# Token and state loads of later batches rearranged over two DMA queues, and one batch's attention chain placed two steps earlier

## The chip, the cores and the metric

The kernel runs on one core of a Trainium2 chip. The metric is the device time of one execution in microseconds (us). Before the change the median of three runs is 204.96 us (204.93 to 205.63).

## The reference

Eight batches of cross attention between 512 tokens and 32 state vectors per head (8 heads of width 64), in both directions, then one feed-forward layer over all 8 × 544 rows:

```python
scores = scale * x @ state.T            # [B, H, 512, 32], softmax over the 32 states
xread  = softmax(scores) @ state        # [B, H, 512, 64]
scores2 = scale * state @ x.T           # [B, H, 32, 512], softmax over the 512 tokens
sread  = softmax(scores2) @ x           # [B, H, 32, 64]
rows   = concat([xread, sread], axis=2) # to [B * 544, 512]
h = rows @ w_in                         # w_in [512, 2048]
out = maximum(0.01 * h, h) @ w_out      # w_out [2048, 512]
```

Inputs and output are fp32.

## The kernel before

The kernel works in bf16 on TensorE with fp32 sums. It does not form `xread`: for each batch it first multiplies the states with w_in (`a_m`, the matrix M, four column groups of 512, each copied out of PSUM by `m_evict`), so that the first feed-forward matmul is attention weights times M.

The order of the instructions on each engine is written out by hand; nothing is scheduled afterwards. SP and Pool each issue DMAs from their own instruction stream, in order, and an instruction that has to wait holds what is behind it.

Per batch the work is:
- load of the tokens, fp32 (`load_x`, tile `xl`, one buffer for all batches from 2 on), a cast to bf16 (`cast_x`), and a DMA transpose by SP (`a_xt_dma`, tile `xT`);
- states: `load_state(i)` loads a group of batches (group 0: batches 2 and 3, group 1: batches 4 to 7) with eight small DMAs; `state_t(i)` casts on Pool and transposes by DMA on SP (`st_t`);
- `a_scores` on TensorE into the PSUM tile `sc`; `a_shift` (maxima per row, their transposed spread and the subtraction, on DVE), `a_max2` (maxima of the second softmax), `a_exp` and `a_exp2` on ScalarE (ACT), `a_probs` and `a_probs2` on DVE, which end in the attention weights `aT` and `a2`;
- 16 steps of the first feed-forward matmul (`ff1`, `ff1_pair`): each fills a PSUM bank `ph`, and ACT applies the leaky ReLU into `hT`. `ff1_pair` does two steps in the double bank `big`, which M groups use too;
- the second feed-forward matmul. For batches 0 and 1 it is cut into `piece(b, hT, i, jq)`: quarter jq of the sum for row block i, four matmuls with quarter jq of `w_out`. Later batches use seven products of half size in place of eight (`Batch`, `Fast`).

The steps of one batch are interleaved with the attention of the next and the second matmul of the one before. The change touches the start. The weights are cast in flight by DMAs of Pool in quarters: `w_in` in four (`load_w_in`), `w_out` in four (`load_w_out`). Pool's queue at the start is, in order: the four of w_in, a cast of batch 0, the first quarter of w_out, two halves of batch 1's tokens (`x1`), quarters two to four of w_out, and batch 2's tokens (`load_x(2)`). SP's queue begins with batch 0's tokens in two halves (`xf`); then come the states of batches 2 and 3, held by a small DVE write into their tile that stands behind DVE's casts of batch 1.

Batch 0's attention and first matmul run to about 22 us, then the pieces of batch 0 with w_out's quarters in turn, between which batch 1's transposes, scores and M groups lie. Then comes the loop of 16 steps of batch 1's first matmul, in which at step 5 batch 2's scores and first M group are formed, at step 9 its exp and weights, at steps 11 and 13 its second exp. ACT copies the M group out, and DVE takes one of the output copies.

Of the kernel before, what the change touches and what calls it, by code (L numbers as in the profile page):

```python
# [9 lines left out]
P = 128  # L10
B, H, S, D = 8, 8, 512, 64
# [4 lines left out]
NT = S // P  # L16
NK = H // 2
# [3 lines left out]
FP32 = mybir.dt.float32  # L21
# [6 lines left out]
def kernel(  # L28
# [9 lines left out]
    nc = tc.nc  # L38
# [58 lines left out]
    def load_x(b, eng):  # L97
        xl[b] = xpool.tile([P, H, NT * D], FP32, name="xl", tag="xl", bufs=1)
        eng.dma_start(xl[b][:], x[b].rearrange("h (p t) d -> p h (t d)", t=NT))

    def open_xb(b):
        xs[b] = xpool.tile([P, NT, H, D], BF16, name="xb", tag="xb")

    def cast_x(b, h0, h1, copy):
        copy(  # L105
            xs[b][:, :, h0:h1].rearrange("p t h d -> p h t d"),
            xl[b][:, h0:h1].rearrange("p h (t d) -> p h t d", t=NT),
        )
# [54 lines left out]
    stf = [consts.tile([P, hi - lo, P], FP32, name=f"stf{lo}", tag=f"stf{lo}") for lo, hi in groups]  # L163
    stb = [consts.tile([P, hi - lo, P], BF16, name=f"stb{lo}") for lo, hi in groups]

    def load_state(i):
        lo, hi = groups[i]
        for k in range(NK):
            for g in range(2):
                nc.sync.dma_start(  # L170
                    stf[i][NS * k:NS * (k + 1), :, D * g:D * (g + 1)],
                    state[lo:hi, 2 * k + g].rearrange("b n d -> n b d"),
                )

    def state_t(i):
        POO(stb[i][:], stf[i][:])
        nc.sync.dma_start_transpose(st_t[i][:], stb[i][:].rearrange("p b q -> p (b q)"))
# [6 lines left out]
    def a_open(a, b):  # L184
        a.b = b
        a.xb = xs[b]
        a.xT = att.tile([P, NT, NK, P], BF16, name="xT", tag="xT")
# [69 lines left out]
    def a_exp(a):  # L257
        a.e1 = block_exp(a.sh, NB)
# [5 lines left out]
    def a_max2(a):  # L264
        m2 = att.tile([P, 2], FP32, name="mcol", tag="mcol")
        nc.vector.tensor_reduce(out=m2[:], in_=a.sc[:], axis=AX.X, op=ALU.max, negate=True)  # L266
        a.m2s = att.tile([P, 2], FP32, name="mcols", tag="mcols")
        nc.vector.tensor_scalar(out=a.m2s[:], in0=m2[:], scalar1=SCALE, scalar2=None, op0=ALU.mult)
# [484 lines left out]
    for u in range(2):  # L753
        nc.gpsimd.dma_start(
            x1[u][:], x[1, NK * u:NK * (u + 1)].rearrange("h (p t) d -> p h (t d)", t=NT)
        )
    for c in range(1, 4):
        load_w_out(c)
    load_x(2, nc.gpsimd)
    a0.aT = att.tile([P, 2, S], BF16, name="aT", tag="aT")  # L760
    open_xb(1)
    a_open(a1, 1)
# [63 lines left out]
    for j, tag in ((4, "py"), (6, "sc"), (8, "py"), (10, "ph"), (12, "py"), (14, "ph")):  # L826
        t, bk = open_ff1_0(tag)
        for g in range(2):
            ff1_0(bk, j, g)
        relu0(t, j)  # L830
        if j == 8:
            m_evict(a0, 3, a_m(a0, 3, "big"), VEC)
            a_scores(a0)
            a_max2(a0)
    for u in range(2):
        VEC(
            a1.xb[:, :, NK * u:NK * (u + 1)].rearrange("p t h d -> p h t d"),
            x1[u][:].rearrange("p h (t d) -> p h t d", t=NT),
        )
    nc.vector.memset(stf[0][:, 0, D - 1:D + 1], 0.0)  # L840
    load_state(0)

    for g in range(2):
        a_exp2(a0, g)
# [18 lines left out]
        piece(0, h0, i, 1)  # L863
    m_evict(a1, 2, a_m(a1, 2, "ph"), SCA)
    a_exp(a1)
    for i in (2, 3):
        piece(0, h0, i, 1)
    m_evict(a1, 3, a_m(a1, 3, "ph"), SCA)
    for g in range(2):
        a_exp2(a1, g)  # L870
    open_xb(2)
    state_t(0)
    cast_x(2, 0, 4, SCA)
    cast_x(2, 4, 8, POO)
    a_open(a2, 2)
    a_xt_dma(a2)
    load_x(3, nc.sync)
    open_xb(3)
    a_probs(a1)
# [15 lines left out]
    for s in range(16):  # L895
        if s in (6, 10):
            ff1_pair(a1, h1, s, "big")
        elif s not in (7, 11):
            ff1(a1, h1, s)
        if s == 5:  # L900
            a_scores(a2)
            m_evict(a2, 0, a_m(a2, 0, "big"), SCA)
            a_shift(a2)
            a_max2(a2)
        if s % 2:
            pb, hT, i, jq = fill[s // 2]
            piece(pb, hT, i, jq, copy=VEC if s == 3 else SCA)
        if s == 7:
            a_open(att_of[3], 3)
            a_xt_dma(att_of[3])  # L910
        elif s == 9:
            a_exp(a2)
            a_probs(a2)
        elif s in (11, 13):
            a_exp2(a2, s // 2 - 5)
    a_probs2(a2)
    a_probs2(a1)
    a_a2t(a1)
    pm = [a_m(a2, 1, "big"), a_m(a2, 2, "sc")]
    m_evict(a2, 1, pm[0], VEC)  # L920
    m_evict(a2, 2, pm[1], SCA)

# [2 lines left out]
    for b in range(2, B):  # L927
        hT = hpool.tile([P, 16, S], BF16, name="hT", tag="hT")
        a = att_of[b]
        nxt = att_of[b + 1] if b + 1 < B else None  # L930
        now = Batch(b, hT)
        std = []
        if b == 2:
            std = [(i, 3) for i in range(2)] + [(i, jq) for i in range(2, NT) for jq in range(4)]

        def fill(s):
            n = (PACE2 if b == 2 else PACE)[s]
            left = min(n, len(before.units)) if before else 0
            if left:
                before.run(left)  # L940
            if n > left:
                now.run(n - left)

        for s in range(16):
            if s == 11:
                fill(s)
            ff1(a, hT, s)
            if s == 0:
                if b + 2 < B:
                    load_x(b + 2, nc.sync)  # L950
                    open_xb(b + 2)
                a_a2t(a)
                if before:
                    for n in (0, 1):
                        before.f.sums(n, 4, 8)
            elif s == 1:
                if nxt is not None:
                    a_scores(nxt)
                m_evict(a, 3, a_m(a, 3, "big"), SCA)
                if b == 2:  # L960
                    a_sread_rows([a0])
                if nxt is not None:
                    a_shift(nxt)
                if b + 2 < B:
                    for h in range(0, H, 2):
                        cast_x(b + 2, h, h + 2, POO)
                if before:
                    before.f.sums(2, 4, 8)
            elif s == 3:
                if before:  # L970
                    before.f.sums(3)
                if nxt is not None:
                    a_max2(nxt)
                if b == 2:
                    weights_sum(0)
                    weights_sum(2)
            elif s == 4:
                if b == 2:
                    load_state(1)
                elif b == 4:  # L980
                    sread_t(0, 4)
                elif b == 7:
                    sread_t(1, 3)
            elif s == 8:
                if nxt is None:
                    a_sread(a)
                if b == 2:
                    state_t(1)
                    weights_sum(1)
                    weights_sum(3)  # L990
            elif s == 12:
                for n in range(3):
                    now.f.sums(n, 0, 4)
            if nxt is None:
                if s == 4:
                    fi = FastIn(None)
                    for n in range(3):
                        fi.w_sum(n)
                elif s == 10:
                    fi.w_sum(3)  # L1000
                    fi.x_sums()
            if s == (11 if b == 2 else 7) and b + 2 < B:
                a_open(att_of[b + 2], b + 2)
                a_xt_dma(att_of[b + 2])
            if nxt is not None:
                if s == 5:
                    a_exp(nxt)
                elif s in (7, 8):
                    a_exp2(nxt, s - 7)
                    if s == 7:  # L1010
                        a_probs(nxt)
                elif s == 11:
                    a_probs2(nxt)
                elif s in (12, 13):
                    SCA(nxt.M[:, s - 12, DM:2 * DM], pm1[:, s - 12, :])
            if std:
                i, jq = std.pop(0)
                piece(1, h1, i, jq)
            elif s != 11:
                fill(s)  # L1020
            if s == 10 and nxt is not None:
                a_sread_rows([a1, a2] if b == 2 else [a])
                pm0 = a_m(nxt, 0, "big")
                pm1 = a_m(nxt, 1, "sc")
                pm2 = a_m(nxt, 2, "ph")
                for g, copy in enumerate((VEC, SCA)):
                    copy(nxt.M[:, g, 2 * DM:3 * DM], pm2[g][:])
                m_evict(nxt, 0, pm0, SCA)
        before = now
# [90 lines left out]
```

## Time and profile before

| | |
|---|---|
| median of three runs | 204.96 us |
| the profiled execution | 204.74 us |
| its span | 202.9 us |
| granted TensorE clock | 1.0 |
| TensorE busy | 196.8 us, 97% |
| DVE, ACT, Pool busy | 75%, 71%, 21% |
| moved by DMA | 28.0 MB, 138 GB/s over the span |
| landing of batch 2's tokens after issue | 19.1 us |
| landing of a quarter of w_out, median | 16.9 us |

The span runs from the first to the last instruction on the engines; the profiled execution's own time is 1.8 us longer. A line of a timeline gives the start, the length of the merged group, engine, source line, operation, output <- input, the number of instructions and in brackets the idle time before it and what ended that. PE is TensorE, PEld its weight loads. A DMA's row on an issuing engine is the time of its issue; the landing stands in a part of its own. Matmul ends are modelled, so the distance of starts says more than the busy time.

### The profile page before, as it was taken

To read this page: it belongs to the slowest core of one execution; us is meant where nothing else is said; L and a number is where in the kernel's file an instruction comes from. 1 tells how busy PE (TensorE), PEld (TensorE's weight loads), DVE (VectorE), ACT (ScalarE), POOL (GpSimd) and SP (SyncE) were. 2 spreads that over 40 slices of the span, in tenths; PEclk is the share of its full clock that TensorE was granted. 3 is DMA by queue.
4 is the path that set the end of the run, shared out by engine and by line. 5 is a ranking of instruction groups with operands and counts; after the bars stand their busy time and mean duration, and the time that the engine had idled before them with its cause. 6 is when DMAs were issued, how large, how long until landed. Compare 5 with 4: busy or idle time off the path is not lost.

```text
span 202.9 us, 4755 instructions
## 1 busy us (share of the span) xinstructions
PE 196.8 (97%) x1964; PEld 125.7 (62%) x1964; DVE 152.7 (75%) x231; ACT 143.3 (71%) x264; POOL 42.3 (21%) x66
## 2 busy tenths in 40 slices
PE   7989999999999999999999999999999999999993
PEld 2543534434344567766776767776767677799882
DVE  1767689689999969976997699769968853686612
ACT  3558748579869796978797878788778856467710
POOL 8931002022007004400251040200020002004250
PEclk9999999999999999999999999999999999999999
DMA  5999994799396986538946795250017000410035
GB/s 187 227 207 277 229 252 131 147 304 236 64 265 190 104 183 159 103 117 256 122 30 181 236 131 105 103 158 5 0 50 213 18 0 28 182 55 0 3 89 170
DMA packets 39733, 27.99 MB, mean 138 GB/s; under 512 B 25312, under 2 KB 36704, under 8 KB 39712
## 3 DMA queue, kind: packets, MB, share of 16 engines
q1 hardware_dynamic: 34512, 20.88, 42.9%
q0 software_dynamic: 4912, 6.55, 15.8%
q8 instruction: 15, 0.25, 0.5%
q10 hardware_dynamic: 288, 0.26, 0.5%
q14 instruction: 6, 0.05, 0.1%
HBM read 17.30 MB, written 8.91 MB: 129 GB/s over the span
## 4 chain that ended last, share of the span: by engine, by line
PE 89%; DMA 5%; POOL 2%; ACT 1%; DVE 1%; issue 0%; POOLq 0%
PE yq L557 36%; PE ph L372 23%; PE py L487 10%; DMA w_in_bf<-in_moe_w_in_dram 5%; PE pm L351 4%; PE pyw L487 3%; PE pf L441 3%; PE yu L557 3%; PE ph L803 2%; PE psn L318 1%; PE sc L206 1%; PE phw L383 1%; POOL w_in_bf L118 1%; DVE M L365 1%; ACT hT L377 1%; ACT M L365 1%
## 5 line engine op out<-in xcount | busy, mean ns | idle before, releaser
L377 ACT ACTIVATE hT<-ph 128x512 bf16<-128x512 f32 x108 | 63.6, 604 | 22.0 <-PE ph L372 21.5
L372 PE MATMUL ph<-aT,M 128*128 128x512 bf16 x216 | 62.3, 379 | 0.0
L557 PEld LDWEIGHTS <-su 128*128 128x128 bf16 x416 | 39.7, 98 | 14.5 <-DVE su L546 1.7
L557 PEld LDWEIGHTS <-hT 128*128 128x128 bf16 x288 | 27.7, 98 | 11.8 <-issue 1.1
L105 POOL CAST xb<-xl 128x512 bf16<-128x512 f32 (+1 forms) x21 | 16.4, 818 | 61.1 <-DMA xl<-in_x_dram 61.1
L557 PE MATMUL yq<-tw_xf,su 128*128 128x256 bf16 x192 | 27.2, 273 | 0.0
L557 PE MATMUL yq<-w_out_bf,hT 128*128 128x256 bf16 x192 | 27.0, 273 | 0.0
L372 PEld LDWEIGHTS <-M 128*128 128x128 bf16 x216 | 21.0, 98 | 9.1 <-DVE r L280 0.4
L546 DVE TENSOR_TENSOR su<-hT 128x1024 bf16<-128x1024 bf16 x24 | 16.9, 702 | 10.5 <-ACT hT L377 10.5
L487 PE MATMUL py<-w_out_bf,hT 128*128 128x512 bf16 x96 | 24.2, 380 | 0.0
L487 PEld LDWEIGHTS <-hT 128*128 128x128 bf16 x128 | 12.0, 98 | 14.8 <-issue 1.3
L627 POOL TENSOR_TENSOR yo<-sv,sv 128x512 f32<-128x512 f32 x6 | 7.8, 1300 | 52.8 <-ACT sv L566 41.3
L569 DVE TENSOR_TENSOR yo<-yq,sv 128x512 f32<-128x512 f32 x17 | 11.6, 685 | 6.5 <-PE yq L557 6.5
L566 ACT COPY sv<-yq 128x512 f32<-128x512 f32 x24 | 13.9, 585 | 2.0 <-PE yq L557 1.4
L365 ACT CAST M<-pm 128x1024 bf16<-128x1024 f32 x13 | 13.2, 1014 | 0.6 <-PE pm L351 0.6
L557 PE MATMUL yq<-w_out_bf,su 128*128 128x256 bf16 x96 | 13.1, 273 | 0.0
L557 PE MATMUL yq<-tw_x,su 128*128 128x256 bf16 x96 | 13.1, 273 | 0.0
L557 PE MATMUL yq<-tw_x,hT 128*128 128x256 bf16 x88 | 12.1, 273 | 0.0
L274 ACT ACTIVATE e<-sc,mcols 128x512 bf16<-128x512 f32 x16 | 11.1, 696 | 0.0
L216 DVE TRANSPOSE_TENSOR_REDUCE mrow<-sc 128x32 f32<-128x1024 f32 x7 | 8.7, 1243 | 1.4 <-PE sc L206 1.4
L266 DVE TENSOR_REDUCE mcol<-sc 128x2 f32<-128x1024 f32 x8 | 9.7, 1214 | 0.0
L224 DVE STREAM_TRANSPOSE mrowb<-mrow 128x1024 f32<-128x1024 f32 x7 | 8.7, 1245 | 0.2
(148 smaller groups left out, 271.5 us busy)
## 6 DMA issues: line engine op xcount, KB each, us to landing
xl<-in_x_dram SPq DMA_DIRECT2D x5, 1024.0 KB, 6.8
out_dram<-yo SPq DMA_DIRECT2D x10, 512.0 KB, 2.8
w_in_bf<-in_moe_w_in_dram POOLq DMA_DIRECT2D x4, 512.0 KB, 8.9
w_out_bf<-in_moe_w_out_dram POOLq DMA_DIRECT2D x4, 512.0 KB, 16.9
out_dram<-ysb SPq DMA_DIRECT2D x8, 256.0 KB, 5.4
xf<-in_x_dram SPq DMA_DIRECT2D x2, 512.0 KB, 4.8
x<-in_x_dram POOLq DMA_DIRECT2D x2, 512.0 KB, 14.0
xl<-in_x_dram POOLq DMA_DIRECT2D x1, 1024.0 KB, 19.1
```

Of the source, the lines that this page charges most:

```text
L105: copy(xs[b][:, :, h0:h1].rearrange("p t h d -> p h t d"), xl[b][:, h0:h1].rearrange("p h (t d) -> p h t d", t=NT),)
L216: nc.vector.tensor_reduce(out=m1[:], in_=flat.rearrange("p (c j) -> p c j", j=NS), axis=AX.X, op=ALU.max, apply_transpose=True,)
L266: nc.vector.tensor_reduce(out=m2[:], in_=a.sc[:], axis=AX.X, op=ALU.max, negate=True)
L274: nc.scalar.activation(out=a.e2[:, g], in_=a.sc[:, g, :], func=AF.Exp, bias=a.m2s[:, g:g + 1], scale=SCALE, accum_out=a.r2[:, g:g + 1],)
L365: copy(a.M[:, :, cols], pm[:])
L372: nc.tensor.matmul(ph[:], lhsT=a.M[:, g, P * j:P * (j + 1)], rhs=a.aT[:, g, :], start=(g == 0), stop=(g == 1),)
L377: nc.scalar.activation(out=hT[:, j, :], in_=ph[:], func=AF.Prelu, alpha=0.01)
L487: nc.tensor.matmul(y.py, lhsT=hT[:, j, P * i:P * (i + 1)], rhs=w_out_bf[:, j, :], start=(j == 0), stop=(j == 15),)
L546: (eng or nc.vector).tensor_tensor(out=S[n][:, ms], in0=u[:, ms], in1=v[:, ms], op=op)
L557: nc.tensor.matmul(bank[:, i, :], lhsT=lhs[:, m, P * i:P * (i + 1)], rhs=rhs[:, m, :], start=(first and m == 0 and (i == 0 or of is not No ...
L566: copy(t[:], bank)
L569: nc.vector.tensor_tensor(out=dst, in0=bank, in1=self.sv[n][:], op=ALU.add)
```

## The change

- Batch 2's tokens no longer stand at the end of Pool's queue. They are loaded by SP in two halves, right behind batch 0's tokens, and are held by a small DVE write into their tile, which stands after batch 0's second maxima and ahead of batch 1's casts.
- The eight loads of the states of batches 2 and 3 move from SP to Pool, between batch 1's tokens and w_out's second quarter. Their DVE write is dropped.
- The casts of batch 2 (ACT, Pool) and its transpose move up: on ACT the cast now stands behind batch 1's exp, ahead of its last M copies and second exps.
- In batch 1's loop the scores and first M group of batch 2 go from step 5 to step 3, its exp and weights from step 9 to 7, its second exps from 11 and 13 to 9 and 11. The output copy of step 3 goes from DVE to ACT.
- The states of batches 4 to 7 are loaded in that loop, four DMAs at step 5 and four at step 9, in place of step 4 of the next one; their cast and transpose move from step 8 to step 4 there. Batch 4's token transpose goes from step 11 to 9.
- After the loop, the normalisation `a_probs2` and transpose of batch 1's second softmax stand behind the two M copies of batch 2.

```diff
-    def load_state(i):
+    def load_state(i, ks=range(NK), eng=nc.sync):
...
-        for k in range(NK):
+        for k in ks:
...
-                nc.sync.dma_start(
+                eng.dma_start(
...
         nc.gpsimd.dma_start(
             x1[u][:], x[1, NK * u:NK * (u + 1)].rearrange("h (p t) d -> p h (t d)", t=NT)
         )
+    load_state(0, eng=nc.gpsimd)
     for c in range(1, 4):
         load_w_out(c)
-    load_x(2, nc.gpsimd)
...
             a_scores(a0)
             a_max2(a0)
+    xl[2] = xpool.tile([P, H, NT * D], FP32, name="xl", tag="xl", bufs=1)
+    nc.vector.memset(xl[2][:].rearrange("p h q -> p (h q)")[:, NK * NT * D - 1:NK * NT * D + 1], 0.0)
+    for u in range(2):
+        nc.sync.dma_start(
+            xl[2][:, NK * u:NK * (u + 1)],
+            x[2, NK * u:NK * (u + 1)].rearrange("h (p t) d -> p h (t d)", t=NT),
+        )
...
-    nc.vector.memset(stf[0][:, 0, D - 1:D + 1], 0.0)
-    load_state(0)
+
+    state_t(0)
...
     a_exp(a1)
+    open_xb(2)
+    cast_x(2, 0, 4, SCA)
+    cast_x(2, 4, 8, POO)
+    a_open(a2, 2)
+    a_xt_dma(a2)
     for i in (2, 3):
         piece(0, h0, i, 1)
     m_evict(a1, 3, a_m(a1, 3, "ph"), SCA)
     for g in range(2):
         a_exp2(a1, g)
-    open_xb(2)
-    state_t(0)
-    cast_x(2, 0, 4, SCA)
-    cast_x(2, 4, 8, POO)
-    a_open(a2, 2)
-    a_xt_dma(a2)
...
-        if s == 5:
+        if s % 2:
+            pb, hT, i, jq = fill[s // 2]
+            piece(pb, hT, i, jq)
+        if s == 3:
             a_scores(a2)
             m_evict(a2, 0, a_m(a2, 0, "big"), SCA)
             a_shift(a2)
             a_max2(a2)
-        if s % 2:
-            pb, hT, i, jq = fill[s // 2]
-            piece(pb, hT, i, jq, copy=VEC if s == 3 else SCA)
         if s == 7:
+            a_exp(a2)
+            a_probs(a2)
             a_open(att_of[3], 3)
             a_xt_dma(att_of[3])
-        elif s == 9:
-            a_exp(a2)
-            a_probs(a2)
-        elif s in (11, 13):
-            a_exp2(a2, s // 2 - 5)
+        elif s in (9, 11):
+            a_exp2(a2, s // 2 - 4)
+        if s in (5, 9):
+            load_state(1, range(s // 2 - 2, s // 2))
     a_probs2(a2)
-    a_probs2(a1)
-    a_a2t(a1)
     pm = [a_m(a2, 1, "big"), a_m(a2, 2, "sc")]
     m_evict(a2, 1, pm[0], VEC)
     m_evict(a2, 2, pm[1], SCA)
+    a_probs2(a1)
+    a_a2t(a1)
...
                 if b == 2:
-                    load_state(1)
+                    state_t(1)
...
-                    state_t(1)
...
-            if s == (11 if b == 2 else 7) and b + 2 < B:
+            if s == (9 if b == 2 else 7) and b + 2 < B:
```

## The prediction

> **What bounds the kernel now.** I read the page first.
>
> ```profile
> span 202.9 us, 4755 instructions
> ...
> PE 196.8 (97%) x1964; PEld 125.7 (62%) x1964; DVE 152.7 (75%) x231; ACT 143.3 (71%) x264; POOL 42.3 (21%) x66
> ```
>
> TensorE is busy 97% of the span, and the change alters no matmul, only their order. So it can win no more than the holes in PE's row, and any matmul that it makes wait costs its full wait: PE takes its instructions in order, and everything behind it shifts. Second I read PE's timeline for holes in the stretch that the change touches, then ACT's beside it.
>
> ```profile
> 40.82 0.41 PE L206 MATMUL sc<-xT,st_t 64*32 64x512 bf16 x8
> 41.03 0.41 PE L351 MATMUL pm<-w_in_bf,st_t 64*32 64x512 bf16 x8
> 41.38 1.04 PE L487 MATMUL py<-w_out_bf,hT 128*128 128x512 bf16 x4
> 42.64 1.02 PE L383 MATMUL phw<-aT,M 128*128 128x512 bf16 x4 [0.22 <-ACT M L365]
> 43.50 1.03 PE L487 MATMUL py<-w_out_bf,hT 128*128 128x512 bf16 x4
> ...
> 41.57 1.01 ACT L365 CAST M<-pm 128x1024 bf16<-128x1024 f32 x1
> ```
>
> Four matmuls of this shape occupy 0.86 us from start to start (42.64 to 43.50), so the group of 41.38 should hand over at 42.24; phw starts at 42.64. That hole of 0.40 us is the largest between 20 and 66 us: phw needs the bank "big", which ACT's copy of batch 2's M frees at 42.58. This is what "two steps up" can win.
>
> Third I read Pool's queue, since the change puts eight transfers into it.
>
> ```profile
> 3.00 3.18 POOL L118 DMA_DIRECT2D w_in_bf<-in_moe_w_in_dram  x4
> ...
> 7.38 0.75 POOL L124 DMA_DIRECT2D w_out_bf<-in_moe_w_out_dram  x1
> 8.12 1.52 POOL L754 DMA_DIRECT2D x<-in_x_dram  x2
> 9.61 1.53 POOL L124 DMA_DIRECT2D w_out_bf<-in_moe_w_out_dram  x2
> 11.74 0.74 POOL L124 DMA_DIRECT2D w_out_bf<-in_moe_w_out_dram  x1 [0.59 <-DMA w_in_bf<-in_moe_w_in_dram]
> 15.29 0.90 POOL L99 DMA_DIRECT2D xl<-in_x_dram  x1 [2.81 <-DMA w_in_bf<-in_moe_w_in_dram]
> ```
>
> The bracketed idles are the key. Neither the last quarter of w_out nor xl reads w_in; they wait because Pool's transfers share eight completion counters in turn, and one may be issued only when the transfer eight places before it has landed. The tenth waits for the second (w_in's second quarter, 11.4), the eleventh for the third (15.0).
>
> Fourth, the landings: w_in's four quarters, x1's two halves, w_out's four quarters, and w_out's second quarter alone (asked for over its issue).
>
> ```profile
> DMA to landing us min/median/max: 5.9/8.9/12.2
> ...
> DMA to landing us min/median/max: 13.7/14.0/14.3
> ...
> DMA to landing us min/median/max: 12.9/16.9/19.7
> ...
> w_out_bf<-in_moe_w_out_dram POOLq DMA_DIRECT2D x1, 512.0 KB, 16.0
> ```
>
> With the issue times: w_in's fourth lands at 5.40+12.2=17.6, w_out's first at 7.38+12.9=20.3, x1 at 8.12+13.7=21.8 and 8.87+14.3=23.2, w_out's second at 9.61+16.0=25.6.
>
> Last, who needs w_out's second quarter: the pieces behind batch 1's second M group.
>
> ```profile
> 26.84 1.90 PE L487 MATMUL py<-w_out_bf,hT 128*128 128x512 bf16 x8
> ...
> 31.19 1.90 PE L487 MATMUL py<-w_out_bf,hT 128*128 128x512 bf16 x8
> 32.92 3.62 PE L487 MATMUL pyw<-w_out_bf,hT 128*128 128x512 bf16 x16
> ```
>
> The quarters two, three and four are needed at 26.84, 31.19 and about 34.65 (eight slots of 0.216 into the last row). The second has 1.2 us to spare.
>
> **States on Pool's queue: the cost.** Eight small transfers (32 partitions, 16 KB each) now stand between x1 and w_out's second quarter. They are numbers 8 to 15 of Pool's transfers, so by the rule of eight the first is free and the others wait for w_in 1 to 4, w_out's first and x1's halves; w_out's second quarter is the sixteenth. Pool wakes about 0.3 us after a landing (11.4 to 11.74, 15.0 to 15.29). One such issue takes about 0.5 us (Pool's own 64 KB stores at L1060: 496 to 548 ns). So:
> - state loads 1 to 3 go at 9.6, 10.1 and 11.7; the fourth at 15.3, the fifth at 17.9, the sixth at 20.6, the seventh at 22.1, the eighth at 23.2+0.3=23.5, done at 24.0;
> - w_out's second quarter is issued at 24.0 instead of 9.61, into an empty queue; the third and fourth at 24.7 and 25.5.
>
> Its time to land there: the trace has one quarter issued into an empty Pool queue, w_in's first: 5.9 us, with x0's megabyte of SP running beside it until 6.0. That gives 29.9. The lower end is put together: a 64 KB store of Pool lands in 1.9 to 2.2 us (page, part 6: 2.1); a quarter of w_out has eight times its bytes, 2.5 us of data (the step from w_out's second landing, 25.6, to its third: 10.35+17.8=28.15, where 17.8 lies as far above the median of 16.9 as 16.0 below it), so 2.0+2.5×7/8=4.2 us, landing at 28.2. I take 5.1, landing at 29.1, between the two: batch 2's x from SP runs beside it as x0 did beside w_in, but for less of it. PE stands still from 26.84 to 29.1: **2.2 us** (1.3 to 3.0), and all matmuls behind it with it. In that time ACT waits too: batch 1's third M group comes after the stalled pieces, and ACT's exp of batch 1 is queued behind its copy. The exp moves from 30.59 to about 32.3, the attention weights from 36.04 to about 38.1; the first ff1 of batch 1 wants them at 36.38+2.2=38.6, so no second wait.
>
> The other quarters: landings at 31.6 and 34.1, or 0.8 each later if they are slowed as the fourth is now by SP's traffic (25.6, 28.15, 31.4: steps of 2.5 and 3.3); needed at 33.4 and 36.9. Covered.
>
> The Trainium skill bears on this issue. "SBUF — State Buffer", section "SBUF: two separate sides", says that a fast-mode copy on the vector engine locks Pool out of its port, so that it cannot write the descriptors of its DMAs. Here DVE casts the second half of x1 (0.69 us from 23.22) just when the last state load is due. By the rule Pool would lose up to 0.5 us more and the sum would be 0.5 higher; the trace's Pool issues (0.75 to 0.92 each) neither show nor exclude it.
>
> **Batch 2's x on SP: nothing.** The load leaves Pool's queue end (landed at 15.29+19.1=34.4) and goes to SP behind a DVE write that follows batch 0's maxima (21.4). At x0's 4.3 us for half a megabyte, both halves land near 27. ACT takes its cast after batch 1's exp, at about 33.3, Pool later than 26.2, when its issues are over. The transpose of batch 2's x then goes at about 34.4 and lands 5.1 us later (as now: issued at 35.65), at 39.5; the scores want it at 39.83+2.2. Hidden. ACT's cast now stands ahead of batch 1's last M copy (1.05 us), whose banks ff1 wants only at 38.6: hidden. If x came after 34, ACT would hold those copies and the same ff1; that would cost its lateness.
>
> **The chain two steps up: the gain.** Scores and first M group of batch 2 go from step 5 to step 3. M's copy then runs at about 40.75 to 41.75 (old clock) while phw comes at 42.46, after ff1 4 and 5 and a piece: the hole of **0.40** closes. The y copy of step 3 goes from DVE (0.69) to ACT (0.58), ahead of M's copy, and ends by 40.6 before M's matmuls do: hidden. Should M's copy be late, the 0.40 is not won; that is the lower bound of the gain.
>
> **States of 4 to 7 earlier, other moves: nothing.** Eight SP issues of about 0.45 us each (four ahead of batch 3's x transpose, four behind) move from 58.8 up to step 5 and 9. Batch 3's scores are at 53.75 and its transpose is issued at 46.77: 1.8 us ahead of it fit. The two normalisations swapped with an M copy on DVE feed a transpose used at 67. Batch 4's x transpose at step 9 instead of 11 has slack to 74.92.
>
> **The sum.** The profiled execution took 204.74 us, span 202.9; 204.74 − 0.40 + 2.2 = 206.5. The median of the three runs shown is 0.2 above that execution, so I give 206.7 against 204.96.
>
> **The rivals.**
> - *w_out arrives in time.* If its second quarter lands within 2.9 us of the issue at 24.0, or the eight waits don't hold it, PE does not stop, the 0.40 remains: 204.3 to 204.6, not slower. For it: eight small loads, and an idle queue. Against it: 2.5 us of data alone, and the two waits seen in Pool's timeline. 0.12. The Trainium skill, "DMA: Bandwidth & Descriptors", section "Anatomy of one DMA — SWDGE (gpsimd) path", fits 2.0 us plus bytes over 436 GB/s. For 0.5 MB that is an estimate of 3.2 us and a stall of 0.3, a sum of 204.6; the 5.9 of w_in's first quarter speaks against it.
> - *A larger hole.* Pool's last issues are held beside DVE's cast, or SP's load of x slows x1 and w_out: 0.5 to 1.5 more, 207.2 to 208.2. For it: w_out's fourth quarter took 0.8 more beside SP's loads. Against: x should be through by 27. 0.13.
> - *The gap stays.* ACT, with one copy more, frees the bank late: 207.1 with the stall. 0.08, inside the range.
> - *A real gain.* The holes in PE's row from 20 to 66 us that the change can reach are 0.4 us, so over 0.5% (1.0 us, about what a measurement of this kernel can tell from no change) would need work that I don't see: 0.03.
>
> **How the numbers follow.** The forecast has the rest, 0.64, with 205.8 to 207.6 by its bounds. The range goes from 205.5, a stall of about 1.1, to 208.2, the larger hole; it leaves out the case in time and the real gain. Slower by over 0.5% means a stall above about 1.4: most of the forecast, all of the larger hole and the open gap, 0.79 in all; within 0.5%: the case in time and the low end of the forecast, 0.18; faster 0.03.
>
> **What would show it.** Pool's timeline with state loads issued at 11.7, 15.3, 17.9, 20.6, 22.1 and 23.5, and w_out's second quarter at about 24; PE idle ahead of the py group at 26.84 with w_out's DMA as releaser, 1.3 to 3.0 us; phw without a hole; everything behind shifted by one constant. I am wrong if w_out's second quarter is issued before 20, if PE's py group starts at 26.84, or if the shift at 66 us differs from the stall less 0.4.

## The result, and the profile after

After the change the kernel takes 211.12 us (median; 209.50 to 211.54), beside 205.20 us (204.93 to 205.63) for the kernel before on the same chip: a ratio of 1.027, with a 95% interval from 1.023 to 1.031. The forecast was 206.7, in a range from 205.5 to 208.2. The direction and the place of the loss were right; the loss is 5.9 us where 1.7 were forecast. The profiled execution of after is one of its shorter ones, 209.78 us with a span of 208.0; what follows accounts for that one, and the others have no trace. All six executions show the same mean granted clock, 0.992.

The page of after, its span, the busy time of the engines, and the granted clock in 40 slices:

```profile
span 208.0 us, 4725 instructions
...
PE 197.0 (95%) x1939; PEld 126.2 (61%) x1964; DVE 151.5 (73%) x230; ACT 143.6 (69%) x265; POOL 43.4 (21%) x73
...
PEclk9999996999999999999999999999999999999999
```

The busy time of TensorE is about as it was (196.8 before; the trace of after lacks 25 of the 1964 matmul records) and the span is 5.1 longer, so the loss is time in which PE stands still or runs slowly. The seventh slice of the clock shows a 6: a row that the prediction did not look at.

The waits of PE, with the total, the number and the longest:

```profile
PE py L487 <- DMA w_out_bf<-in_moe_w_out_dram: 3.2, 1, 3.2
PE pspin L132 <- DVE warm L71: 1.2, 1, 1.2
PE pst L150 <- DVE stb L649: 0.5, 1, 0.5
...
```

One wait is new and large: the pieces with w_out's second quarter. The wait of 0.5 at L150 is in batch 0's opening, before anything that the change touches.

Pool's timeline, from its issue of batch 1's tokens on:

```profile
8.50 1.53 POOL L754 DMA_DIRECT2D x<-in_x_dram  x2
9.99 1.11 POOL L170 DMA_DIRECT2D stf<-in_state_dram  x2
12.82 0.54 POOL L170 DMA_DIRECT2D stf<-in_state_dram  x1 [1.72 <-DMA w_in_bf<-in_moe_w_in_dram]
15.32 0.54 POOL L170 DMA_DIRECT2D stf<-in_state_dram  x1 [1.96 <-DMA w_in_bf<-in_moe_w_in_dram]
17.86 0.54 POOL L170 DMA_DIRECT2D stf<-in_state_dram  x1 [2.00 <-DMA w_in_bf<-in_moe_w_in_dram]
20.50 0.54 POOL L170 DMA_DIRECT2D stf<-in_state_dram  x1 [2.10 <-DMA w_out_bf<-in_moe_w_out_dram]
21.99 0.81 POOL L170 DMA_DIRECT2D stf<-in_state_dram  x1 [0.96 <-DMA x<-in_x_dram]
23.54 0.54 POOL L170 DMA_DIRECT2D stf<-in_state_dram  x1 [0.74 <-DMA x<-in_x_dram]
24.07 2.29 POOL L124 DMA_DIRECT2D w_out_bf<-in_moe_w_out_dram  x3
```

Each state load is released by the transfer eight places before it, in the order w_in, w_in, w_in, w_out's first quarter, x1, x1. W_out's second quarter goes at 24.07, forecast at 24.0.

Its landing, asked for over that issue, and PE's timeline there:

```profile
w_out_bf<-in_moe_w_out_dram POOLq DMA_DIRECT2D x1, 512.0 KB, 6.7
```

```profile
27.21 0.40 PE L351 MATMUL pm<-w_in_bf,st 64*32 64x512 bf16 x8
30.84 0.38 PE L487 MATMUL py<-w_out_bf,hT 128*128 128x512 bf16 x1 [3.22 <-DMA w_out_bf<-in_moe_w_out_dram]
31.44 2.77 PE L487 MATMUL py<-w_out_bf,hT 128*128 128x512 bf16 x6 [0.22 <-issue]
34.13 0.56 PE L351 MATMUL pm<-w_in_bf,st 64*32 64x512 bf16 x8
...
47.83 1.03 PE L383 MATMUL phw<-aT,M 128*128 128x512 bf16 x4
```

The quarter lands at 24.07+6.7=30.8, and the pieces start there. They then take 3.29 us from start to start (30.84 to 34.13) for eight matmuls, one of them without a record, that took 1.73 at 0.216 each. The stretches of PE's row say why (busy, matmuls, granted clock, DMA share, GB/s):

```profile
30.00:31.00 1.00, 0.17 (x1) 1.00 1.21 186
31.00:32.00 1.00, 0.78 (x3) 0.54 1.21 200
32.00:33.00 1.00, 1.00 (x4) 0.50 1.21 197
33.00:34.00 1.00, 1.00 (x3) 0.50 1.22 176
34.00:35.00 1.00, 1.00 (x11) 0.76 1.33 207
```

The clock was granted at half from about 31.1, just behind the start of the first matmul, until about 34.5, and in that time matmuls start 0.427 us apart. The last line of PE's timeline answers to the 0.40 us hole of before: phw has no bracket.

The account, by the start of the same matmul after and before: +0.70 already at batch 0's scores (19.32 against 18.62; the first loads, which the change does not touch, and later kernels with the same start had −0.03 to +0.38 there); +3.30 more at the stalled pieces (30.84 against 26.84 is 4.00); +1.60 by batch 2's stretch, for the half clock; −0.38 for the hole; −0.1 at batch 4's scores; +5.12 at the end.

### The profile page after: what moved, and what is told of

It reads as the page before. It is cut to its first block, busy times and chain, and to the rows that moved or that the text cites. A ratio compares the mean times of both kernels' runs of the same rounds, so it can differ in the third digit from the quotient of the medians.

```text
span 208.0 us, 4725 instructions
## 1 busy us (share of the span) xinstructions
PE 197.0 (95%) x1939; PEld 126.2 (61%) x1964; DVE 151.5 (73%) x230; ACT 143.6 (69%) x265; POOL 43.4 (21%) x73
## 4 chain that ended last, share of the span: by engine, by line
PE 81%; DMA 13%; issue 1%; POOL 1%; DVE 1%; ACT 0%; SPq 0%; POOLq 0%
PE yq L557 35%; PE ph L372 21%; PE py L487 10%; DMA x<-in_x_dram 7%; PE pm L351 3%; DMA w_out_bf<-in_moe_w_out_dram 3%; PE pf L441 3%; PE yu L557 3%; DMA xf<-in_x_dram 3%; PE pyw L487 3%; PE psn L318 1%; PE sc L206 1%; PE phw L383 1%; DVE su L546 1%; PE yz L557 0%
## 5 line engine op out<-in xcount | busy, mean ns | idle before, releaser
L372 PE MATMUL ph<-aT,M 128*128 128x512 bf16 x199 | 59.7, 379 | 0.3
L557 PEld LDWEIGHTS <-hT 128*128 128x128 bf16 x288 | 27.7, 98 | 11.8 <-issue 1.1
L105 POOL CAST xb<-xl 128x512 bf16<-128x512 f32 (+1 forms) x21 | 14.4, 724 | 74.3 <-DMA xl<-in_x_dram 43.9
L487 PE MATMUL py<-w_out_bf,hT 128*128 128x512 bf16 x92 | 25.1, 396 | 3.8 <-DMA w_out_bf<-in_moe_w_out_dram 3.2
L487 PEld LDWEIGHTS <-hT 128*128 128x128 bf16 x128 | 12.5, 100 | 18.7 <-issue 5.6
L238 DVE TRANSPOSE_TENSOR_REDUCE r<-e 128x32 f32<-128x1024 bf16 x7 | 8.7, 1239 | 4.2 <-ACT e L233 4.2
```

The source lines that it names most:

```text
L105: copy(xs[b][:, :, h0:h1].rearrange("p t h d -> p h t d"), xl[b][:, h0:h1].rearrange("p h (t d) -> p h t d", t=NT),)
L372: nc.tensor.matmul(ph[:], lhsT=a.M[:, g, P * j:P * (j + 1)], rhs=a.aT[:, g, :], start=(g == 0), stop=(g == 1),)
L487: nc.tensor.matmul(y.py, lhsT=hT[:, j, P * i:P * (i + 1)], rhs=w_out_bf[:, j, :], start=(j == 0), stop=(j == 15),)
L557: nc.tensor.matmul(bank[:, i, :], lhsT=lhs[:, m, P * i:P * (i + 1)], rhs=rhs[:, m, :], start=(first and m == 0 and (i == 0 or of is not No ...
```

## The experiments

A shift below is the start of a matmul less the start of the same one in the profiled execution of before. Between its start (batch 0's scores) and its end it is free of what differs in the first loads.

**Without the idle time: e1_fill and e6_fill22.** Is it the half clock that costs 1.6 us? Ahead of the pieces with w_out's second quarter, matmuls of a tile of zeros are added to the open sum; they change nothing in it, and keep PE busy while the quarter lands. E1 has 14 of them, e6 22.

```diff
+    for _ in range(14):
+        nc.tensor.matmul(ys[0, 0].py, lhsT=idle[:, :P], rhs=idle[:], start=False, stop=False)
     for i in (0, 1):
         piece(0, h0, i, 1)
```

> The changed kernel with 14 matmuls of a zero tile, added into the bank that the stalled piece sums in, right ahead of that piece; they add nothing to the sum and last about as long as TensorE now waits (3.2 us). Theory of the clock: the wait for w_out's second quarter costs twice, once as idle time and once because the eight matmuls behind it run at half clock (0.427 us from start to start where 0.216 is usual). Then the granted clock stays at 1.0 from 31 to 34 us, those eight pieces and the M group behind take 1.6 us less, and the time falls by 1.6 us, to about 209.5 median. Rival: the half clock has nothing to do with the idle time (a general limit in that stretch); then the rows from 31 to 34 stay at 0.5 and the time stays at 211.

> The changed kernel with 22 zero matmuls (4.75 us) in place of 14 ahead of the stalled piece, so that TensorE is idle there for under 1 us. Theory of the clock: with no idle stretch left the clock never falls, and the second group of times that the changed kernel has (209.5 to 209.8 and 211.1 to 211.5) goes with it: all runs within 208.8 to 209.8. Rival (the upper group comes from DMA landings, not from the clock): two groups 1.5 us apart remain.

E1 took 209.64 (209.36 to 211.80; ratio 1.025, interval 1.019 to 1.030), e6 209.66 (208.94 to 210.24; 1.022, 1.020 to 1.024). PE's timeline and the granted clock behind the wait of e1:

```profile
31.97 1.89 PE L487 MATMUL py<-w_out_bf,hT 128*128 128x512 bf16 x8 [1.91 <-DMA w_out_bf<-in_moe_w_out_dram]
```

```profile
32.00:34.00 2.00, 2.00 (x16) 1.00 1.20 184
```

And PE's timeline of e6:

```profile
32.48 1.89 PE L487 MATMUL py<-w_out_bf,hT 128*128 128x512 bf16 x8 [0.49 <-DMA w_out_bf<-in_moe_w_out_dram]
```

The clock stays at 1.00, and the group takes 1.81 us in e1 where it took 3.29. That is 1.5 us, and the medians agree (211.12 less 209.65 is 1.5, though from different comparisons, with before at 205.20 and at 204.92 and 205.16). The profiled executions alone do not show it in the end time: the quarter, issued at 24.63 in e1 and 23.96 in e6, lands 7.3 and 8.5 us later, against 6.7 in after, and from start to end they shift by 4.7 and 4.9, against 4.4 in after; what the clock saved went into a later landing. So with the same order in the queues this landing varies by 1.8 us between three traces.

The runs without a trace say something too. The longest of e1's four, 211.80, has a mean granted clock of 0.992, as after's six have; the other three, 209.36 to 209.92, have 0.998 to 1.000. So e1's filling did not keep the clock every time, and the run that lost it is 1.9 us or more longer. All four of e6 have 0.999 or 1.000, so what is left of their spread, 1.3 us (one of them lies above the expected range), is not the clock's. That it is the landing's is what the three traces suggest; it is not shown.

The Trainium skill, "TensorE: Matmul & The Clock Gate", section "Part 1: The HAM clock gate", gives half the clock after an idle window of about 3.4 us, and the full one after as much of sustained work, with a window that runs free. The traces agree in size: 3.22 us of idle time in after (3.60 from start to start), then 3.4 us at half; and with 1.91 idle in e1's nothing. In e3's trace below, the clock falls at about 29.8 (a mean of 0.94 from 28 to 30), 2.9 us after the last matmul's modelled end (26.52+0.40), so there somewhat less than the 3.4 was enough.

**Where the quarter's landing comes from: e3_x_pool.** Batch 2's tokens go back to the end of Pool's queue; all else is as in after (one load of 1 MB in place of two halves, without the DVE write).

```diff
     for c in range(1, 4):
         load_w_out(c)
+    load_x(2, nc.gpsimd)
...
-    xl[2] = xpool.tile([P, H, NT * D], FP32, name="xl", tag="xl", bufs=1)
...
-        nc.sync.dma_start(
-            xl[2][:, NK * u:NK * (u + 1)],
-            x[2, NK * u:NK * (u + 1)].rearrange("h (p t) d -> p h (t d)", t=NT),
-        )
```

> The changed kernel with batch 2's tokens back at the end of Pool's queue (all eight states still ahead of w_out's second quarter). To be read at the landing of w_out's second quarter, issued at 24.1 as now, with nothing of SP beside it. Theory S: it lands 4.2 to 5.0 us after its issue, at 28.3 to 29.1, in place of 6.7 us (30.8), and TensorE's wait there falls from 3.2 to about 1.2 us. Theory Q alone: 6.7 us again. The whole time says less: the tokens land at about 36, ACT's cast of them stands ahead of copies that batch 1's first matmul needs, and a second wait of 1 to 2 us comes there under both theories.

It took 209.88 (two runs, 209.53 and 210.23; 1.024, 1.020 to 1.027). The landing of the quarter, PE's timeline, and the stretches around the end of the wait:

```profile
w_out_bf<-in_moe_w_out_dram POOLq DMA_DIRECT2D x1, 512.0 KB, 6.0
```

```profile
26.52 0.40 PE L351 MATMUL pm<-w_in_bf,st 64*32 64x512 bf16 x8
30.57 3.17 PE L487 MATMUL py<-w_out_bf,hT 128*128 128x512 bf16 x8 [3.65 <-DMA w_out_bf<-in_moe_w_out_dram]
```

```profile
28.00:30.00 2.00, 0.00 (x0) 0.94 1.04 149
30.00:32.00 2.00, 1.43 (x4) 0.50 1.04 166
```

The quarter, issued at 24.56, lands after 6.0 us with no tokens on SP beside it: neither the 4.2 to 5.0 of theory S (SP's tokens slow the quarter) nor the 6.7 of theory Q (Pool's queue alone makes it late). So most of the landing is there without SP, and 6.0 is close to the 5.9 of w_in's first quarter in before. Its first packet moves at about 25.9, 1.3 us after the issue, though nothing but a small state load stood in its way; behind it come Pool's next two quarters. Beside SP's tokens it took 0.7 (after) to 2.5 (e6) more, in one trace each. The other run of e3 has no trace; its mean granted clock is 1.000, beside 0.989 in this one.

**Fewer loads ahead of the quarter: e2_four and e4_four_late.** In e2, four of the eight state loads stand ahead of w_out's second quarter and four behind its fourth. E4 is e2 with the loads of batch 2's tokens later on SP, behind DVE's second copy of batch 1's transposes.

```diff
-    load_state(0, eng=nc.gpsimd)
+    load_state(0, range(2), nc.gpsimd)
     for c in range(1, 4):
         load_w_out(c)
+    load_state(0, range(2, 4), nc.gpsimd)
```

And in e4, with the same lines taken out ahead of batch 1's casts:

```diff
         piece(0, h0, 2 + u, 0, bank=wide[:, u])
+    xl[2] = xpool.tile([P, H, NT * D], FP32, name="xl", tag="xl", bufs=1)
...
+        nc.sync.dma_start(
+            xl[2][:, NK * u:NK * (u + 1)],
+            x[2, NK * u:NK * (u + 1)].rearrange("h (p t) d -> p h (t d)", t=NT),
+        )
+    state_t(0)
     a_scores(a1)
```

> The changed kernel with four of the eight state loads ahead of w_out's second quarter on Pool's queue and four behind its last. The second quarter is then Pool's 12th transfer and waits for the 4th (w_in's last, landed at 17.6), so it is issued at about 17.9 in place of 24.1, while the queue still works on batch 1's tokens. Theory Q (the counters of Pool's queue alone make the quarter late): it lands by about 26, TensorE does not wait, no half clock; 204.6. Theory S (SP's load of batch 2's tokens, moving from 23.0 to 27.5, keeps the DMA engines from the quarter whenever it is issued): it lands at 28 to 29, TensorE waits 1.5 to 2.5 us; 206 to 207.

> As the kernel with four states ahead, and SP's load of batch 2's tokens held until DVE's second copy of batch 1's transpose (about 26.2), with the states' transpose behind it on SP. Theories Q and S together: w_out's second quarter lands by 26, the third by 28.5, the fourth near 34, TensorE waits for none of them, and the hole ahead of phw is closed: 204.5. If S is wrong and Q right, it is as fast as the kernel with four states ahead. If w_out's fourth quarter is pushed behind 34.6 by the tokens, a small wait of up to 1 us shows ahead of the piece at 34.6 (205.5).

E2 took 206.27 (206.09 to 207.90; 1.009, 1.006 to 1.012). Its timelines of Pool, of SP and of PE:

```profile
17.72 0.78 POOL L124 DMA_DIRECT2D w_out_bf<-in_moe_w_out_dram  x1 [2.76 <-DMA w_in_bf<-in_moe_w_in_dram]
...
35.51 0.52 POOL L176 CAST stb<-stf 128x256 bf16<-128x256 f32 x1 [9.92 <-DMA stf<-in_state_dram]
35.98 1.04 POOL L105 CAST xb<-xl 128x1024 bf16<-128x1024 f32 x1
```

```profile
37.47 2.58 SPq L190 DMA_TRANSPOSE xT<-xb  x1
```

```profile
42.03 0.41 PE L206 MATMUL sc<-xT,st_t 64*32 64x512 bf16 x8 [1.90 <-DMA xT<-xb]
```

The quarter goes at 17.72, into a queue that still holds w_out's first quarter and batch 1's tokens, and lands at 26.0: its stall of 3.2 and the half clock are gone in this trace. What is late next is batch 2. SP's tokens, issued at 21.57, moved their first byte at 25.1, and their halves took 8.9 and 12.7 us to land; Pool's cast of the states waited for the last of the state loads until 35.51, its cast of the tokens stood behind that, and the scores waited 1.90 for the transpose. So e2's time lies in the range of theory S by chance: the quarter came in time, as theory Q had it, and the wait is at a place that neither named.

E4 took 204.98 (204.56 to 205.85; 1.000, 0.999 to 1.002). PE's timeline of e4:

```profile
40.65 0.41 PE L206 MATMUL sc<-xT,st_t 64*32 64x512 bf16 x8 [0.68 <-DMA xT<-xb]
```

So half of the state loads ahead of the quarter cost nothing at the quarter, and tokens that start after it leave 0.68 at the scores, which is more than the hole's 0.38.

**How far the quarter may go back: e8_six.** Six state loads ahead of it, two behind; the diff is against e2.

```diff
-    load_state(0, range(2), nc.gpsimd)
+    load_state(0, range(3), nc.gpsimd)
...
-    load_state(0, range(2, 4), nc.gpsimd)
+    load_state(0, range(3, 4), nc.gpsimd)
```

> The changed kernel with six state loads ahead of w_out's second quarter and two behind the last. The quarter waits for Pool's sixth transfer (batch 1's first half, 21.8) and is issued at 22.1, about when the queue runs empty (22.5). Theory Q as it stands now (a quarter that is issued into an empty Pool queue takes 6.0 to 7.3 us, whatever SP does): it lands at 28.1 or later, TensorE waits 1.2 us or more there; with the wait for batch 2's transpose behind it 206 to 207.5. Rival (only the time of the issue counts, with 4 to 5 us for the landing): it lands at 26.5 to 27, hardly any wait there, 205 to 206.3.

It took 207.72 (207.55 to 208.50, three runs; 1.013, 1.011 to 1.014), 3.4 us less than after and just above the range of theory Q; the rival's range lies lower. Two more runs took 211.07 and 212.44. The profile is that of the longest, so the place of its wait is read and not its price. PE's timeline:

```profile
32.38 3.57 PE L487 MATMUL py<-w_out_bf,hT 128*128 128x512 bf16 x8 [5.15 <-DMA w_out_bf<-in_moe_w_out_dram]
```

The quarter was issued at 22.44, 1.6 us earlier than in after, and in this execution landed after 9.9, later than there. Between 26.5 and 30.5 SP's tokens and Pool's queue moved about 100 packets per us each. A time of issue alone does not say when a transfer lands: e2's quarter stood in the queue behind batch 1's tokens, whose last half landed at about 23.2, and followed them after 2.8 us, about the step of a full queue; e8's was issued just as the data in Pool's queue ran out (about 22.5) and SP's megabyte began. That this is the reason is argued from these two traces; the three shorter runs of e8 have none.

**The chain alone: e7_chain.** Kernel before, with the scores, first M group, exp and second exps of batch 2 two steps up and the output copy of step 3 on ACT; both queues are as before.

```diff
-        if s == 5:
+        if s == 3:
             a_scores(a2)
...
-        elif s == 9:
+        if s == 7:
             a_exp(a2)
             a_probs(a2)
...
-        elif s in (11, 13):
-            a_exp2(a2, s // 2 - 5)
+        elif s in (9, 11):
+            a_exp2(a2, s // 2 - 4)
```

> The kernel before with the chain of batch 2 two steps up alone (scores and first M group at step 3, exp at 7, second exps at 9 and 11, the y copy on ACT); both queues as before. The transpose of batch 2's tokens lands at 40.75, the scores would start at 39.8: TensorE waits 0.95 us for it, and the hole of 0.40 ahead of phw closes. Theory (the steps earn their 0.4 only when the tokens come earlier): 0.55 us slower than before, 205.45. Rival (the chain's steps are free): 0.4 less, 204.5.

It took 205.54 (205.37 to 206.25; 1.003, 1.002 to 1.004). PE's timeline:

```profile
41.19 0.41 PE L206 MATMUL sc<-xT,st_t 64*32 64x512 bf16 x8 [0.90 <-DMA xT<-xb]
```

A wait of 0.90 for the transpose takes the place of the 0.40 ahead of phw: +0.49 from start to end. The chain needs the earlier tokens, which is what the moved loads are good for.

**All state loads on SP: e10_states_sp.** After, with the eight state loads on SP behind batch 2's tokens, and none on Pool; the cast and transpose of the states move behind those of the tokens.

```diff
-    load_state(0, eng=nc.gpsimd)
     for c in range(1, 4):
         load_w_out(c)
...
             x[2, NK * u:NK * (u + 1)].rearrange("h (p t) d -> p h (t d)", t=NT),
         )
+    load_state(0)
...
-    state_t(0)
...
     a_xt_dma(a2)
+    state_t(0)
```

> The kernel after, with the eight state loads taken off Pool and put on SP right behind batch 2's tokens (their cast and transpose behind those of batch 2's tokens); Pool then issues w_out's second quarter right behind batch 1's tokens, as before the change. Theory that only the place of the state loads on Pool costs time: w_out's second quarter is issued at 9.6 and lands by 26.8 or with a wait under 0.5, no time at half clock, and the chain two steps up keeps its 0.38: 204.8 to 205.3. Rival: tokens and states of batch 2 on SP from 21.5 to 30 slow w_out's quarters by more than their slack of 1.2 us, or arrive late themselves for the scores that now come at 40.5: 205.8 to 207.

It took 205.50 beside 204.99 (204.75 to 206.39; 1.002, 1.000 to 1.003), 0.2 above the range of its theory. Pool issues the second and third quarter at once, there is no wait for w_out and no half clock. In PE's timeline the scores wait for the states, as the rival's second half had it:

```profile
9.84 1.54 POOL L124 DMA_DIRECT2D w_out_bf<-in_moe_w_out_dram  x2
```

```profile
40.90 0.41 PE L206 MATMUL sc<-xT,st_t 64*32 64x512 bf16 x8 [0.70 <-DMA st_t<-stb]
```

Of after's 5.9 us, 5.4 are gone with the state loads off Pool: their place ahead of the quarter is the cause. What is left, the rest of the change with the states on SP, comes to no difference that the times can tell.

**The hole by itself: e5_pair8, e9_pair8_probs2, e11_joined.** Can the 0.40 be won without the loads? E5 is the kernel before with the double steps of batch 1's first matmul, which need the bank "big", at 8 and 12. E9 also copies batch 2's second M group ahead of batch 1's second normalisations, as the change does. E11 also takes the change's places for the state loads, cast and transpose of batches 4 to 7, and batch 4's token transpose at step 9.

```diff
-        if s in (6, 10):
+        if s in (8, 12):
             ff1_pair(a1, h1, s, "big")
-        elif s not in (7, 11):
+        elif s not in (9, 13):
             ff1(a1, h1, s)
```

In e9 and e11 in addition:

```diff
-    a_probs2(a1)
-    a_a2t(a1)
     pm = [a_m(a2, 1, "big"), a_m(a2, 2, "sc")]
     m_evict(a2, 1, pm[0], VEC)
     m_evict(a2, 2, pm[1], SCA)
+    a_probs2(a1)
+    a_a2t(a1)
```

And in e11:

```diff
+        if s in (5, 9):
+            load_state(1, range(s // 2 - 2, s // 2))
...
-            if s == (11 if b == 2 else 7) and b + 2 < B:
+            if s == (9 if b == 2 else 7) and b + 2 < B:
```

> The kernel before, with nothing of the change; only the two double steps of batch 1's first matmul move from steps 6 and 10 to 8 and 12, so that steps 6 and 7 use the single banks and do not wait for the bank big that ACT's copy of batch 2's M frees at 42.58. It puts a price on the hole alone. Theory (the hole ahead of phw is worth 0.4 us and nothing behind it takes it back): 0.4 us less than before, 204.5. Rival (the hole is made up for elsewhere, or ACT's single steps open another): no change, 204.9.

> Kernel before, with the double steps of batch 1's first matmul at 8 and 12 instead of 6 and 10, and in addition DVE's copy of batch 2's second M group ahead of the normalisations of batch 1's second softmax. Theory: the hole of 0.40 us ahead of phw closes as it did with the double steps moved alone, and is no longer lost again at batch 2's next M group, since the copy that group waited for comes 1.2 us or more earlier: 204.8, 0.38 below before. Rival: the order behind the loop is not what gave it back, and the next tight place is another one: 205.1 to 205.2 as with the double steps alone, with the wait at another line.

> Kernel before with the queues of its start untouched, the double steps of batch 1's first matmul at 8 and 12, DVE's M copy ahead of batch 1's second normalisations, and the change's own places for the state loads of batches 4 to 7, their cast and transpose, and batch 4's token transpose. Theory: the hole of 0.40 us was given back at batch 4's scores, whose token transpose was issued 2.7 us later because SP held the transpose of batch 1's second softmax ahead of it; with the state loads gone from that stretch and the transpose at step 9 no wait is left there, and the whole 0.38 stays to the end: 204.6 against 205.0, a shift of -0.4 between the start and the end of the profiled run. Rival: SP's state loads in batch 1's loop make batch 3's transpose late, a wait of 0.2 to 0.6 ahead of batch 3's scores at 53.75, and the time is 204.9 to 205.3.

E5 took 205.05 beside 205.16 (1.000, 0.999 to 1.000), e9 205.17 beside 204.99 (1.001, 1.000 to 1.003), e11 204.67 beside 204.94 (0.999, 0.997 to 1.000). The one wait of PE that is new in the timeline of e5, and the one in that of e9:

```profile
54.33 0.41 PE L351 MATMUL pm<-w_in_bf,st_t 64*32 64x512 bf16 x8 [0.17 <-DVE M L365]
```

```profile
75.33 0.41 PE L206 MATMUL sc<-xT,st_t 64*32 64x512 bf16 x8 [0.47 <-DMA xT<-xb]
```

In e5 the shift goes from +0.38 at 40.82 to 0.00 at 53.75 and back to +0.36 behind the wait at batch 2's next M group. In e9 that place is free (−0.04 at 67), and the time is given back at batch 4's scores: SP issued that transpose at 70.78 instead of 68.11, since it stood behind the second softmax's transposes that were now later. So in both the rival's forecast came true. In e11 no wait of PE is there that was not there before, and its profiled execution has +0.29 at the start and −0.22 at the end, 0.51 less. The waits of PE in e11:

```profile
PE pspin L132 <- DVE warm L71: 1.2, 1, 1.2
PE sct L674 <- ACT xT L666: 0.3, 1, 0.3
PE qb L695 <- DVE q L731: 0.2, 1, 0.2
PE r L721 <- DVE q L731: 0.2, 1, 0.2
```

The median is 0.27 lower, and the interval of the ratio just holds 1: the trace shows the gain, and the times of twelve runs do not settle it; the start alone varies by 0.4 between the traces of these kernels. No other kernel here has a median more than 0.11 below before (e5).

## Why the prediction was wrong

- **What bounds the kernel.** Right: TensorE's row; the whole loss is one wait of PE and what followed it.
- **Pool's queue.** Right, to 0.1 us: the rule of eight, read from two brackets of before, gave 15.3, 17.9, 20.6, 22.1, 23.5 and 24.0; measured 15.32, 17.86, 20.50, 21.99, 23.54 and 24.07. One was late, 12.82 for 11.7 (w_in's second quarter landed later), without effect.
- **The landing: the term that was mis-sized.** The step took 5.1 us, halfway between a built-up 4.2 and the 5.9 of the one quarter that the trace shows going into an empty queue. Measured: 6.7, and 6.0 even without SP's tokens (e3). The measured row was the nearer one, and an upper end was missing: with tokens on SP beside it the traces have 6.7 to 8.5. The stall was 3.30 for a forecast of 2.2 (1.3 to 3.0). The built-up price added 64 KB stores to a step of 2.5 us between landings in a full queue; that step is what a queue gives once it is going.
- **The clock: the term that was missing.** "All matmuls behind it with it" was priced as a shift alone. The idle time let the clock fall to half, which cost another 1.6 (e1: 1.5). Whether the forecast's own 2.2 would have cost it stays open. In the traces of e1 and e2 an idle time of 1.9 left the clock alone; but by their mean granted clock of 0.992 (0.996 and more in every run of before) one of e1's four runs and two of e2's seven, 207.64 and 207.90, lost it too, and these have no trace. The prediction's test "wrong if the shift at 66 us differs from the stall less 0.4" found it: stall 3.30 less 0.4 is 2.9, and the shift there is 5.22−0.70=4.5.
- **The hole.** The number was right: phw without a wait and −0.38. That it stays won was luck as far as the reasoning goes, since other edits of the change, counted as nothing, seem to keep it: in kernels that close the hole by other means it is given back further on without the M copy ahead of the normalisations (e5), and without the earlier loads of states 4 to 7 and transpose of batch 4 (e9 beside e11).
- **Tokens on SP, states 4 to 7, copies.** Right: SP issued the tokens from 22.14 on and the second half had landed at 28.0 (forecast near 27), the transpose went at 37.80, and the scores did not wait. E7 shows what the moved tokens are worth to the chain, 0.9; the prediction counted them at nothing, correctly for the sum.
- **The rivals.** "In time" fell, with the estimate of 3.2 us by the Trainium skill's "DMA: Bandwidth & Descriptors", section "Anatomy of one DMA — SWDGE (gpsimd) path": measured 6.0 to 8.5 behind an empty queue, so the measurement decides against it here. In "a larger hole" the half that named SP's tokens was right in kind. The half with DVE's lock on Pool (the Trainium skill's "SBUF — State Buffer", section "SBUF: two separate sides") is not seen: the last state load, beside DVE's cast of 23.28 to 23.97, took 0.54 like those beside none; one at 21.99, beside the other cast, took 0.81, or 0.27 more, but in e1 and e3 that one, beside the same cast, took 0.54.
- **The median.** The 0.2 us carried from profile to median was that of before. After's median is 1.3 above its own profile; the landing that PE now waits for varies between traces, which may be why, and the clock is the same in all six runs.

## What to carry to other kernels

When a load that TensorE waits for is moved back in a queue, ask first whether the queue still holds work when it is issued: behind batch 1's tokens the quarter followed after 2.8 us (e2), while into an empty queue it took 6.0 and more, and longer when SP had begun a load. Price it by the measured row nearest in kind, not by a sum that comes out lower. Then ask how long TensorE will stand idle: 3.2 us cost half as much again through the half clock here, and of the kernels with about 1.9 some runs lost the clock too. If the stall can't be removed, matmuls of zeros into the open sum can keep the clock. And a hole closed early is won only when every later wait with slack near zero has moved with it.

## What the runs showed of the hardware

- SP's loads start late beside a full Pool queue: from issue to first byte batch 2's tokens took 1.0 us in after, where Pool's queue was almost empty, and 3.6 in e2 and 2.6 in e4, where it was full. Eight state loads of 16 KB took SP 3.6 us to issue in before and 11.3 in e10, behind a megabyte of tokens and beside a full Pool queue.
- A quarter of w_out lands 6.0 us after its issue into an empty queue with nothing of SP beside it (e3), and 6.7, 7.3 and 8.5 beside a megabyte of SP (after, e1, e6); in before's full queue the second and third follow each other by 2.5 us.
- With 3.2 us (after) and 3.7 us (e3) without matmuls the granted clock was 0.50 for 3.4 us, and with 5.2 us (the longest run of e8) for 6.8 us; in traces with 1.9 us (e1, e2) and less it stayed at 1.00.
- In these kernels Pool issues a transfer only when the one eight places before it has landed: in after the fourth to eighth state loads went at 15.32, 17.86, 20.50, 21.99 and 23.54, behind the landings of w_in's third and fourth quarters, w_out's first and batch 1's tokens.
